# Swapping quarters of turned attention operands: GpSimd's copies in place of its transfers

## The chip, the cores and the metric

One core of one Trainium2 chip runs the kernel. The metric is device microseconds of one execution. The kernel before takes 556.05 us as the median of three runs (554.33 to 557.03).

## The reference

Sigmoid attention over 4 batches and 12 heads (448 positions, head size 64), then two gated MLPs with a spatial product, all in float32:

```python
scores = scale * np.matmul(q, k.transpose(0, 1, 3, 2)) - np.log(S)
attn = 1.0 / (1.0 + np.exp(-scores))
attn_out = np.matmul(attn, v)                    # then heads side by side: x is 4 x 448 x 768
h = np.maximum(x @ w_in, 0.0)                    # the first MLP; the second has gelu and g_ln
u, v = h[..., :512], h[..., 512:]
v_n = (v - mu) / np.sqrt(var + 1e-06)
v_s = np.einsum('ts,bsd->btd', w_spatial, v_n) + b_spatial[None, :, None]
x = (u * v_s) @ w_out                            # the second MLP returns x + (u * v_s) @ w_out
```

## The kernel before

The program runs in one order that is written out by hand: attention first (up to 137 us), then the first MLP, a merge of two weight matrices, and the second MLP. Only attention is touched.

Attention works on 12 groups of 4 heads. Each group has 7 units (chunks of 64 key positions), so there are 84 units, numbered s. Unit s does four score matmuls (`scores`, line 464) on four quarters of the systolic array, ScalarE takes the sigmoid (line 470), and three units later four matmuls apply the values (`values`, line 482).

The score matmuls need q and k with the head dimension on partitions. `turn(n)` (line 407) makes this for group n. VectorE transposes 32x32 blocks of the loaded tile `in` into two tiles `op0` and `op1` (line 398, four instructions). Block transposes leave quarters of 32 partitions in the wrong place, so both tiles are copied whole into two spare tiles `t0` and `t1` (line 416), and four quarters are then brought back to other partitions: `op0[32:64]` from `t1[0:32]`, `op1[0:32]` from `t0[32:64]`, and the same again 64 partitions on (`swaps`, line 400). For group 1 VectorE does these four copies (line 419). For groups 2 to 11 GpSimd's queue issues them as DMA transfers (line 421), forty in all. Group 0 has a path of its own, `turn_first`, which uses copies of VectorE, ScalarE and GpSimd (lines 434 to 441). Matmul `(x, o)` of a unit reads partitions 64o to 64o+63 of `op{x}`, in the order x0o0, x0o1, x1o0, x1o1.

`turn(1)` is issued at unit 0, `turn(n + 2)` at the third unit of group n. The `op` tiles have three buffers, the `t` tiles one: the whole copies of one turn (line 416) wait until the quarters of the turn before have been read out of `t`.

Between the turns VectorE works on a belt of 18 jobs (`convert_early`, line 162), which make float32 weights of MLP 1 out of float64 ones: load (line 168 or 170), five integer instructions (lines 175, 178, 181, 185, 190), then for 14 of them a rounded copy and a difference (lines 198, 199), and for the last four a store to `flat` in HBM (line 195). The order of VectorE's instructions is fixed, so a turn and the belt's jobs push each other. Tiles `we` and `fe` of the belt have three buffers each; SyncE issues the loads in order.

At the end of attention `operands_made` (line 850) closes the pool `apool`, which holds `in`, `op`, `t`, `we` and `fe`, and the MLP's pools take its space. The first instruction there (`split_x`, line 574, on ScalarE) makes the first operand of the MLP and waits for the last users of that space, the belt's last store among them. VectorE makes the lower halves (line 575).

Of the kernel before, what the change touches and what calls it, by code (L numbers as in the profile page):

```python
# [26 lines left out]
def tile_sigmoid_attention_two_gated_mlps(  # L27
# [32 lines left out]
    nc = tc.nc  # L60
# [292 lines left out]
    def attention(apool, epool, ps_att, ps_last, done):  # L353
# [27 lines left out]
        def operands(n):  # L381
            ops[n] = [
                apool.tile([P, 2, S], F32, tag=f"op{x}", name=f"op{x}", bufs=3) for x in range(2)
            ]
            return ops[n]

        def spares():
            return [apool.tile([P, 2, S], F32, tag=f"t{x}", name=f"t{x}", bufs=1) for x in range(2)]

        def transpose(t, w, src, j=0, chunks=slice(0, None)):  # L390
            src = src.rearrange("p (c j d) -> p j c d", c=TC, j=2)[:, j]
            dst = t[:, w]
            if w:
                src = src.rearrange("p (e c) d -> p c e d", c=KC)[:, chunks]
                dst = dst.rearrange("p (c t e) -> p c e t", c=KC, e=2)[:, chunks]
            else:
                dst = dst.rearrange("p (c t) -> p c t", c=TC)
            nc.vector.transpose(out=dst, in_=src)

        def swaps(ts, us):  # L400


            for at in (0, 64):
                yield ts[0][at + 32:at + 64], us[1][at:at + 32]
                yield ts[1][at:at + 32], us[0][at + 32:at + 64]

        def turn(n):


            ts = operands(n)  # L410
            for j, t in enumerate(ts):
                for w in range(2):
                    transpose(t, w, ins[n][:, w], j)
            us = spares()
            for t, u in zip(ts, us):
                nc.vector.tensor_copy(out=u, in_=t)
            for dst, src in swaps(ts, us):
                if n == 1:
                    nc.vector.tensor_copy(out=dst, in_=src)
                else:  # L420
                    nc.gpsimd.dma_start(out=dst, in_=src)  # L421

        def turn_first():

# [107 lines left out]
        for s in range(U + LAG):  # L532
            n, c = divmod(s, KC)
            if s < U:
                scores(n, c)
            elif s == U:
                done()
            if s in sums:
                values(*sums[s])
            if s == 0:  # L540
                turn(1)
            if c == 2 and n + 2 < NG:
                turn(n + 2)
            if c == 5 and n + 3 < NG:
                load(n + 3)
            if c == 0 and 0 < n < NG - 1:
                load_v(n + 1)
            if s % 2 == 0:
                belt.tick(rate(s // 14, s % 14 // 2))
            if s == U:  # L550
                load_vecs(l1)
            if s >= U and (s - U) % 2 == 0:
                spatial.tick(1)
# [504 lines left out]
```

## Time and profile before

| | us |
|---|---|
| median of three runs | 556.05 |
| lowest, highest | 554.33, 557.03 |
| the profiled execution | 553.84 |
| its span, first to last instruction | 552.1 |
| TensorE busy | 546.1 |
| VectorE busy | 343.8 |
| ScalarE busy | 220.4 |
| GpSimd busy | 55.4 |

The page of the profile gives busy time by engine and in 40 slices. The chain of work that ended last is followed back from the last instruction; the timeline gives the instructions of an engine in order of time, with the idle time before one and what ended it; the waits are summed by pairs of lines. The granted TensorE clock is 1.0 throughout.

### The profile page before, as it was taken

The page shows a single profiled execution, that of the slowest core. Times are in us where ns is not written, and L with a number is a line of the kernel's source. Part 1 is how long each engine was busy: PE and PEld are TensorE (multiplying, and loading weights), DVE is VectorE, ACT ScalarE, POOL GpSimd, SP SyncE. Part 2 cuts the span into 40 slices and gives each one's busy share as a digit, 9 for nine tenths or more (in the row PEclk, how much of TensorE's full clock was granted, in tenths as well). Part 3 has the DMA queues.
Part 4 walks back from the last instruction along what each step waited for, and adds up shares of the span by engine and source line. Part 5 has one row for each costly group of instructions (what it writes and reads, how often), then busy time and mean ns, then how long its engine had stood idle before and what let it go on. Part 6 is the DMA issues. An engine that isn't in the chain of part 4 may idle for free.

```text
span 552.1 us, 8964 instructions
## 1 busy us (share of the span) xinstructions
PE 546.1 (99%) x3398; PEld 448.5 (81%) x3398; DVE 343.8 (62%) x734; ACT 220.4 (40%) x371; POOL 55.4 (10%) x104
## 2 busy tenths in 40 slices
PE   8999999999999999999999999999999999999997
PEld 5356666666899898898998889998999899989886
DVE  6559788793588799999674877932541264225311
ACT  5767777878242352452533245311320142113001
POOL 1112121110210200201100021001000120010000
PEclk9999999999999999999999999999999999999999
DMA  8979989671422454452445534101410032014003
GB/s 281 276 192 243 257 248 263 185 197 52 65 76 96 101 157 116 137 146 88 136 138 117 138 119 132 55 2 20 64 17 1 16 53 33 1 20 67 1 0 115
DMA packets 89547, 61.02 MB, mean 111 GB/s; under 512 B 63776, under 2 KB 77088, under 8 KB 89504
## 3 DMA queue, kind: packets, MB, share of 16 engines
q1 hardware_dynamic: 88080, 55.60, 37.4%
q0 software_dynamic: 1280, 4.59, 3.6%
q8 instruction: 27, 0.44, 0.3%
q10 hardware_dynamic: 144, 0.26, 0.1%
q14 instruction: 16, 0.13, 0.1%
HBM read 44.83 MB, written 11.01 MB: 101 GB/s over the span
## 4 chain that ended last, share of the span: by engine, by line
PE 94%; DMA 3%; DVE 1%; SPq 0%; issue 0%; POOL 0%
PE t L587 17%; PE t L633 17%; PE sc L719 10%; PE av L482 10%; PE sc L464 10%; PE t L653 6%; PE av L719 5%; PE av L653 3%; PE sc L653 3%; PE sc L729 3%; PE t L815 3%; PE av L815 3%; PE av L729 2%; PE t L729 2%; DMA op<-t 1%; DMA in<-in_k_dram 1%
## 5 line engine op out<-in xcount | busy, mean ns | idle before, releaser
L464 PE MATMUL sc<-op 64*64 64x448 f32 x656 | 117.2, 536 | 0.9 <-DMA op<-t 0.9
L482 PE MATMUL av<-a,vt 64*64 64x448 f32 x672 | 118.0, 536 | 0.0
L470 ACT ACTIVATE a<-sc,small 128x896 f32<-128x896 f32 x84 | 84.8, 1013 | 33.9 <-PE sc L464 33.1
L464 PEld LDWEIGHTS sc<-op 64*64 64x64 f32 x656 | 53.2, 133 | 28.4 <-issue 7.1
L482 PEld LDWEIGHTS av<-a,vt 64*64 64x64 f32 x672 | 54.5, 133 | 25.8 <-issue 6.8
L596 DVE BATCH_NORM_STATS2 st<-vr 128x6 f32<-128x512 f32 x28 | 19.4, 694 | 65.2 <-ACT vr L593 65.2
L593 ACT ACTIVATE vr<-t 128x512 f32<-128x512 f32 x28 | 16.7, 598 | 92.6 <-PE t L587 92.5
L598 POOL TENSOR_SCALAR st<-st 128x1 f32<-128x1 f32 x28 | 10.8, 385 | 352.7 <-DVE st L597 322.6
L587 PE MATMUL t<-vh,xh 128*128 128x512 f32 x112 | 41.6, 392 | 0.0
L663 DVE SCALAR_TENSOR_TENSOR gt<-t,bb 128x448 f32<-128x448 f32 x16 | 10.9, 682 | 45.7 <-PE t L653 45.7
L587 PE MATMUL t<-vh,xl 128*128 128x512 f32 x98 | 38.2, 390 | 0.0
L671 ACT CAST gh<-u 128x448 fp32r<-128x448 f32 (+1 forms) x16 | 8.6, 540 | 71.8 <-DVE u L667 71.8
L633 PE MATMUL t<-xh,uh 128*128 128x448 f32 x96 | 34.8, 363 | 0.0
L633 PE MATMUL t<-xh,ul 128*128 128x448 f32 x96 | 34.8, 362 | 0.0
L633 PE MATMUL t<-xl,uh 128*128 128x448 f32 x96 | 34.6, 360 | 0.0
L653 PE MATMUL t<-sh,v 128*128 128x448 f32 x112 | 32.8, 362 | 0.0
L587 PE MATMUL t<-vl,xh 128*128 128x512 f32 x84 | 32.7, 389 | 0.0
L575 DVE TENSOR_TENSOR xl<-x,xh 128x512 fp32r<-128x512 f32 (+1 forms) x32 | 20.0, 654 | 17.1 <-ACT xh L574 16.9
L421 POOL DMA_DIRECT2D op<-t x40 | 21.7, 548 | 83.3 <-PE sc L464 55.0
L633 PE MATMUL t<-xh,vl 128*128 128x448 f32 x96 | 29.6, 362 | 0.0
L638 ACT ACTIVATE u<-t 128x448 f32<-128x448 f32 x32 | 17.4, 544 | 25.2 <-PE t L633 24.9
L615 ACT CAST v<-vr 128x512 fp32r<-128x512 f32 x24 | 14.9, 622 | 30.6 <-DVE vr L607 30.6
(200 smaller groups left out, 1246.4 us busy)
## 6 DMA issues: line engine op xcount, KB each, us to landing
w<-in_moe_w_in_dram SPq DMA_DIRECT2D x24, 256.0 KB, 3.0
in<-in_q_dram SPq DMA_DIRECT2D x12, 448.0 KB, 6.3
vt<-in_v_dram SPq DMA_DIRECT2D x12, 448.0 KB, 6.8
in<-in_k_dram SPq DMA_DIRECT2D x11, 448.0 KB, 7.1
w<-in_moe_w_out_dram SPq DMA_DIRECT2D x18, 256.0 KB, 3.1
op<-t POOLq DMA_DIRECT2D x40, 112.0 KB, 4.9
we<-in_moe_w_in_dram SPq DMA_DIRECT2D x12, 256.0 KB, 8.9
we<-in_moe_w_in_dram SPq DMA_DIRECT2D x16, 192.0 KB, 5.5
```

The lines of the kernel that those rows point to most:

```text
L421: nc.gpsimd.dma_start(out=dst, in_=src)
L464: nc.tensor.matmul(sc[64 * x:64 * x + 64, o, :S], op[x][ps, 1, 64 * c:64 * c + 64], op[x][ps, 0], start=(j == 0), stop=(j == js - 1), tile ...
L470: nc.scalar.activation(a, sc[..., :S], AF.Sigmoid, bias=bias_s, scale=scale)
L482: nc.tensor.matmul(av[o * D:(o + 1) * D, x, :S], vs[n][ps, o, D * c:D * (c + 1)], att[n, c][ps, o], start=(c == 0), stop=(c == KC - 1), ti ...
L575: nc.vector.tensor_tensor(out=pair[1][:, :n], in0=src, in1=raw(pair[0][:, :n]), op=ALU.subtract)
L587: nc.tensor.matmul(ps[:, :FF], a, w, start=(c == 0 and n == 0), stop=(c == self.kc - 1 and n == 2),)
L596: nc.vector.bn_stats(out=st, in_=vr)
L633: nc.tensor.matmul(ps[:, :S], w, a, start=(c == 0 and n == 0), stop=(c == self.kc - 1 and n == 2),)
L653: nc.tensor.matmul(ps[:, :S], a, w, start=(n == 0), stop=(n == len(todo) - 1))
L719: nc.tensor.matmul(self.o[m][:, :n_cols], w, a, start=(not second and i == 0 and n == 0), stop=(second and i == KF - 1 and n == 2),)
L729: nc.tensor.matmul(ps[:, :cols.stop - cols.start], a, w, start=(not second and i == 0 and n == 0), stop=(second and i == KF - 1 and n == 2),)
L815: nc.tensor.matmul(ps[:, :FF], x, w[:, c], start=(c == 0 and n == 0), stop=(c == KD - 1 and n == 2),)
```

## The change

For group 1, VectorE now copies the first and third quarter and GpSimd the second and fourth. For groups 2 to 11, GpSimd copies all four quarters with instructions of its own, and its forty transfers go. Everything else stays: the whole copies into `t`, the order, the buffers.

```diff
-            for dst, src in swaps(ts, us):
-                if n == 1:
-                    nc.vector.tensor_copy(out=dst, in_=src)
-                else:
-                    nc.gpsimd.dma_start(out=dst, in_=src)
+            for i, (dst, src) in enumerate(swaps(ts, us)):
+                engine = nc.vector if n == 1 and i % 2 == 0 else nc.gpsimd
+                engine.tensor_copy(out=dst, in_=src)
```

## Rows read from the trace of the kernel before

**Rows 1.** The page, busy us (share of the span) and instructions by engine.
```profile
PE 546.1 (99%) x3398; PEld 448.5 (81%) x3398; DVE 343.8 (62%) x734; ACT 220.4 (40%) x371; POOL 55.4 (10%) x104
```

**Rows 2.** Timeline of ScalarE: sigmoids of units 13, 14 and 83; start, us, idle before.
```profile
25.99 1.01 ACT L470 ACTIVATE a<-sc,small 128x896 f32<-128x896 f32 x1 [0.52 <-PE sc L464]
30.02 1.01 ACT L470 ACTIVATE a<-sc,small 128x896 f32<-128x896 f32 x1 [3.01 <-PE sc L464]
...
133.74 1.01 ACT L470 ACTIVATE a<-sc,small 128x896 f32<-128x896 f32 x1 [0.50 <-PE sc L464]
```

**Rows 3.** The chain that ended last: start, us, what.
```profile
20.39 7.76 DMA op<-t
```

**Rows 4.** Timeline, turns of groups 2 and 3 and TensorE's unit 14.
```profile
18.77 2.40 DVE L398 STREAM_TRANSPOSE op<-in 128x448 f32<-128x448 f32 x4
19.17 2.22 POOL L421 DMA_DIRECT2D op<-t  x4 [11.40 <-DVE t L416]
...
26.41 0.91 PE L464 MATMUL sc<-op 64*64 64x448 f32 x2
...
29.03 1.16 DVE L416 COPY t<-op 128x896 f32<-128x896 f32 x2 [7.85 <-DMA op<-t]
```

**Rows 5.** Waits, summed: total us, times, longest.
```profile
DVE t L416 <- DMA op<-t: 21.2, 5, 7.9
```

**Rows 6.** Timeline of VectorE: belt instructions behind a turn, and the last turn's copies.
```profile
61.14 0.69 DVE L190 SCALAR_TENSOR_TENSOR fe<-we,fe 128x512 int32<-128x512 int32 x1
61.86 0.43 DVE L198 CAST vh<-fe 128x512 fp32r<-128x512 f32 x1
...
62.93 0.42 DVE L175 TENSOR_SCALAR fe<-we 128x512 int32<-128x512 int32 x1
...
108.88 1.12 DVE L416 COPY t<-op 128x896 f32<-128x896 f32 x2
```

**Rows 7.** Timeline, the belt's end and the start of the MLP.
```profile
126.22 0.56 DVE L190 SCALAR_TENSOR_TENSOR fe<-we,fe 128x384 int32<-128x384 int32 x1
...
126.80 0.32 SPq L195 DMA_DIRECT2D flat<-fe  x1
...
134.65 2.16 ACT L574 CAST xh<-x 128x512 fp32r<-128x512 f32 x4
```

**Rows 8.** Waits of SyncE's queue up to 140 us, and line 195's landing time.
```profile
SPq L320 <- DMA flat<-fe: 1.4, 1, 1.4
...
DMA to landing us min/median/max: 1.8/2.2/3.4
```

**Rows 9.** Timeline in group 0, lines 398, 438 and 441, each copy by itself.
```profile
6.25 0.90 DVE L398 STREAM_TRANSPOSE t<-in 128x320 f32<-128x320 f32 x2
6.49 0.55 POOL L441 COPY op<-t 32x448 f32<-32x448 f32 x1 [5.19 <-DVE op L434]
7.07 0.28 DVE L438 COPY op<-t 128x320 f32<-128x320 f32 x1
7.09 0.68 POOL L441 COPY op<-t 32x448 f32<-32x448 f32 x1
```

**Rows 10.** Lines 438 and 598 by themselves: duration in ns, min/median/max.
```profile
L438 DVE COPY op<-t x2: 283/483/683, 7.1 to 7.3; 128x320 f32<-128x320 f32 x2
...
L598 POOL TENSOR_SCALAR st<-st x28: 221/422/582, 142.9 to 498.2; 128x1 f32<-128x1 f32 x28
```

**Rows 11.** Timeline of GpSimd and VectorE in MLP 1.
```profile
143.16 0.57 POOL L601 TENSOR_TENSOR st<-st,small 128x1 f32<-128x1 f32 x1
...
190.58 0.69 DVE L617 TENSOR_TENSOR v<-vr,v 128x512 fp32r<-128x512 f32 x1
...
190.83 0.87 POOL L601 TENSOR_TENSOR st<-st,small 128x1 f32<-128x1 f32 x1
```

**Rows 12.** Timeline, quarters of group 1 and TensorE's unit 7.
```profile
13.01 2.55 DVE L419 COPY op<-t 32x896 f32<-32x896 f32 x4
...
15.89 0.93 PE L464 MATMUL sc<-op 64*64 64x448 f32 x8
```

## The prediction

> **What bounds the kernel now.** The page first: TensorE is busy for 546.1 of 552.1 us [rows 1], so a change that touches only VectorE, GpSimd and transfers can win no more than TensorE's gaps, but it can open new ones. TensorE's ends are modelled; its gaps in attention are better read from ScalarE, whose sigmoids follow the score matmuls one by one. From unit 14 to unit 83 they start (133.74 - 30.02) / 69 = 1.503 us apart: no gap in 69 units. From unit 13 to unit 14 it is 4.03 us [rows 2]. So attention has one stall of 4.03 - 1.50 = 2.53 us. The chain names its cause: a transfer `op<-t` that ran from 20.39 to 28.15 [rows 3], the swap of group 2, while unit 14 had started its first two matmuls at 26.41 [rows 4].
>
> Then VectorE, which is off the chain. Its timeline is one queue of turns and belt jobs, and the only idle time it shows between 12 and 126 us is five waits of the whole copies (line 416) for the transfers, 21.2 us [rows 5], the longest 7.85 us [rows 4]. It ends its last belt instruction at 126.22 + 0.56 = 126.78; the store is issued at 126.80 [rows 7] and takes about 2.2 us to land [rows 8]: 129.0. The space of `apool` is handed on only then: SyncE's first load into it stood 1.4 us for that store [rows 8]. The first MLP operand starts at 134.65 [rows 7], behind the last sigmoid. VectorE's lateness is thus free up to 134.65 - 129.0 = 5.6 us, and after that it moves the end of attention one for one.
>
> **The change, part by part. Prices.** GpSimd copied 32x448 in 0.55 us beside transposes, and in 0.68 us when a VectorE copy had started just before it. Two VectorE copies of 128x320 lay there: the first took 283 ns, the second, issued while GpSimd copied, 683 ns, so it stood 0.40 us [rows 9, 10]. A GpSimd copy and such a VectorE copy go one after the other here; the transposes (0.90 us for two, beside the first GpSimd copy) did not slow it. The new copies are 32x896, twice as long: 2 x 0.55 = 1.10 us if all of it is per element; if a fixed part as long as GpSimd's shortest one-column instruction, 0.22 us [rows 10], is in it, 0.22 + 2 x 0.33 = 0.88 us. I take 1.0 us.
>
> **The stall of group 2 goes.** The whole copies of group 2 ended about 18.9; four GpSimd copies of 1.0 us end near 22.9, beside transposes only [rows 4]. Unit 14 asks at 26.41, so even (26.41 - 18.9) / 4 = 1.9 us each would do. All later turns start earlier than before, as VectorE's waits shrink too (below). Worth 2.53 us.
>
> **Group 1 loses a little.** VectorE's four copies run from 13.01 to 15.56 and unit 7 starts at 15.89 [rows 12]. Now VectorE and GpSimd take turns: VectorE 13.01, GpSimd from about 13.5, VectorE from 14.4, GpSimd from about 14.9 to 15.9. The fourth quarter then comes 0 us (no turns taken: 13.05 + 2 x 1.0 = 15.05) to 0.6 us late (1.1 us each and turns taken); I take 0.25. TensorE's side of the sum is -2.53 + 0.25 = -2.3 us: the MLP could start at 132.35.
>
> **VectorE's side.** Gone: 21.2 us of waits, and 0.5 us in group 1 (two copies fewer, one wait more). New: the whole copies of group 3 wait for group 2's quarters to be read from `t`, until 22.5, where the transposes are done near 20.7: 1.8 us. Behind them on VectorE stand the belt and all later turns. Without collisions the belt would end at 126.78 - 21.2 - 0.5 + 1.8 = 106.9 at the earliest.
>
> Collisions: behind the copies of each later turn stand belt instructions [rows 6], in part copies and one-input integer instructions (0.43 us for 512 columns, at the copies' speed), in part two-input ones (0.69 us). Does a two-input instruction exclude GpSimd too? A GpSimd instruction of one column takes 0.57 us beside a transpose and 0.87 us where a two-input VectorE instruction of 0.69 us had begun 0.25 us before it [rows 11]; so GpSimd stands behind them. That VectorE's two-input instructions stand behind GpSimd's in turn, no row shows; I take it as symmetric. The Trainium skill (SBUF — State Buffer, "Who interferes with whom") says so: a VectorE instruction with two SBUF inputs contends with a GpSimd instruction that reads SBUF, and the later one blocks fully. By that rule the sum is the one made here; if it did not hold, the first rival below would be.
>
> So VectorE and GpSimd alternate until the four copies are through. Each copy costs VectorE 2 x 0.40 = 0.80 us (0.40 + 0.33 = 0.73 with the fixed part; 0.93, twice the 0.46 us for which the second GpSimd copy kept VectorE out, as the upper end). Group 2's copies lie beside transposes, at nothing; group 3's are followed by four belt instructions and meet three; groups 4 to 11 meet four each: 3 + 32 = 35 collisions, 28.0 us (25.5 to 32.5). The belt ends at 106.9 + 28.0 = 134.9, its store lands at 137.1, and the MLP's first operand starts there and not at 132.35: 137.1 - 134.65 = +2.5 us (0 to +7.0).
>
> On the way the last turn is just in time: its whole copies, before until 110.0 [rows 6], end at 110.0 - 21.2 - 0.5 + 1.8 + 31 x 0.80 = 114.9, its quarters some 5.4 us later at 120.3, and unit 77 asks at 30.02 + 63 x 1.503 - 1.1 - 2.3 = 121.3. The belt's end, not a turn, is what comes last.
>
> The forty transfers leave the DMA engines; TensorE waits for no other load in attention, so this is worth nothing.
>
> **Sum.** 553.84 + 2.5 = 556.3 on the profiled execution (553.8 to 560.8). That execution is 2.2 us under the median. What makes the others longer is not in the trace; if it were later landings of the swaps, it would go, and if not, it stays. I add 0.7: **557.0 us**.
>
> **The rivals.** (1) Two-input instructions don't stand behind GpSimd. Then only lines 198, 175, 178 and 181 collide, with about half of each copy hidden under the others: some 2.1 us a turn, 18 us in all. The belt ends near 125, its store lands by 127.3, under 132.35, and the whole gain stays: 553.84 - 2.3 = 551.5, up to 553.7 with the median's 2.2. For it: VectorE has 26.8 us of room (21.2 + 5.6) ahead of any loss. Against it: the 0.87 us. Chance 0.28. (2) GpSimd's next copy takes the turn as soon as the last ends, and VectorE stands through all four, 4.2 us a turn, 38 us over nine turns: the belt ends near 145, and the MLP starts 12 us late, 566. For it: GpSimd's copies are queued ready; against it: at 7.09 GpSimd got in between two VectorE copies that were equally ready [rows 9]. It decides from 0.85 us a collision on, where the sum passes 558.8. Chance 0.10. (3) The swap is no earlier than by transfer, and the stall of group 2 stays; it needs copies of 1.9 us, nearly twice any row. Then 558.8 or more. Chance 0.02.
>
> **How the numbers follow.** My own case has 0.60. About 0.5% (2.8 us) is what a measurement of this kernel can tell from no change: faster is under 553.3, slower over 558.8. My case gives 0.38 to no change, 0.19 to slower (its upper bounds, and the 2.2 us if common), 0.03 to faster; rival 1 gives 0.19 to faster, 0.09 to no change; rivals 2 and 3 give 0.12 to slower; together, rounded, 0.22, 0.47 and 0.31. The range runs from rival 1 at its best, 551.5, to my upper end with half of the median's surplus, 562; what is left out is rival 2 and the outer ends.
>
> **What would show it.** Right: GpSimd copies of 0.9 to 1.1 us alone and longer beside belt work; belt instructions of 0.43 and 0.69 us stretched to 1.2 to 1.5 us behind each turn; sigmoids 13 and 14 1.5 us apart; the last store after 132 us and the first `xh` waiting for it. Wrong: lines 185, 190 and 199 keep their durations beside GpSimd copies (rival 1), VectorE stands for 3 us at a stretch (rival 2), or TensorE waits inside attention at a later group.

## The result and the profile after

| | before | after |
|---|---|---|
| median, us | 555.54 (6 executions, 554.14 to 558.12) | 551.28 (6 executions, 550.64 to 551.56) |
| the profiled execution, us | 553.84 | 551.56 |
| its span, us | 552.1 | 549.8 |
| TensorE busy, us | 546.1 | 545.0 |
| VectorE busy, us | 343.8 | 364.8 |
| GpSimd busy, us | 55.4 | 79.2 |

The ratio of after to before is 0.9917, 95% interval 0.9891 to 0.9944: faster by 0.8%. The forecast was 557.0, no change or slower. The time came out 0.2 us below the range. (In after.py the lines behind 419 stand 2 lower: sigmoid L468, score matmul L462, first MLP operand L572. The quarters are L419. In e2 and e3 below, the lines from the quarters on stand 2 higher than in before; in e6 most stand 1 lower.)

The page of after, busy time by engine:

```profile
PE 545.0 (99%) x3398; PEld 439.8 (80%) x3398; DVE 364.8 (66%) x732; ACT 220.3 (40%) x371; POOL 79.2 (14%) x106
```

VectorE became 21.0 us busier [rows 1] and the kernel faster. TensorE's busy time fell by 1.1 us of the 2.3 us by which the span fell; its ends are modelled, so the gaps are read from ScalarE.

**Where it went: the gap between units 13 and 14.** Timeline of ScalarE in after, units 13 and 14 (start, duration):

```profile
26.48 1.01 ACT L468 ACTIVATE a<-sc,small 128x896 f32<-128x896 f32 x1 [0.50 <-PE sc L462]
27.99 1.01 ACT L468 ACTIVATE a<-sc,small 128x896 f32<-128x896 f32 x1 [0.50 <-PE sc L462]
```

1.51 us apart where it was 4.03 [rows 2]. The quarters of group 2 now lie on GpSimd, beside transposes. Timelines of GpSimd and VectorE there:

```profile
18.92 3.87 POOL L419 COPY op<-t 32x896 f32<-32x896 f32 x4 [2.57 <-DVE t L416]
...
18.77 2.27 DVE L398 STREAM_TRANSPOSE op<-in 128x448 f32<-128x448 f32 x4
22.82 1.16 DVE L416 COPY t<-op 128x896 f32<-128x896 f32 x2 [1.78 <-POOL op L419]
```

The four copies end at 22.79, 5.4 us before the transfer did [rows 3], and the score matmuls of unit 14 start at 27.14. VectorE's wait of 7.85 us at the next whole copies [rows 4] became 1.78 us. It is the only wait of that kind that is left, in place of 21.2 us [rows 5].

**What it costs on VectorE.** Timeline of VectorE in after, belt instructions behind a turn in the middle of attention, to be held against [rows 6]:

```profile
53.93 0.69 DVE L190 SCALAR_TENSOR_TENSOR fe<-we,fe 128x512 int32<-128x512 int32 x1
54.65 1.04 DVE L198 CAST vh<-fe 128x512 fp32r<-128x512 f32 x1
55.72 1.29 DVE L199 TENSOR_TENSOR vl<-fe,vh 128x512 fp32r<-128x512 f32 x1
56.94 1.15 DVE L175 TENSOR_SCALAR fe<-we 128x512 int32<-128x512 int32 x1
58.12 1.04 DVE L178 TENSOR_SCALAR fe<-fe 128x512 f32<-128x512 f32 x1
59.20 0.43 DVE L181 TENSOR_SCALAR fe<-fe 128x512 int32<-128x512 int32 x1
```

Four instructions in a row are stretched, one for each GpSimd copy, and the fifth is not: the two engines take turns. The stretch is read against the lone durations (0.43, 0.69, 0.42, 0.43): 0.61 + 0.60 + 0.73 + 0.61 = 2.55 us a turn. The forecast had 4 x 0.80 = 3.2. Counted over the whole timeline, 35 belt instructions are stretched, three behind group 3's copies and four behind those of each later group, by 22.4 us together.

**Where it ends.** VectorE's last belt instruction, and the MLP's first operand on ScalarE behind the last sigmoid (timelines of after); then, from its chain, TensorE's last value matmuls and first MLP matmuls:

```profile
128.40 0.56 DVE L190 SCALAR_TENSOR_TENSOR fe<-we,fe 128x384 int32<-128x384 int32 x1
...
131.72 1.01 ACT L468 ACTIVATE a<-sc,small 128x896 f32<-128x896 f32 x1 [0.50 <-PE sc L462]
132.62 2.17 ACT L572 CAST xh<-x 128x512 fp32r<-128x512 f32 x4
...
131.62 3.01 PE av L480 x32
134.63 5.44 PE t L585 x23
```

The belt ends at 128.96. Its store takes 2.1 us to land (1.8 to 2.3 for the four of them): 131.1. That is 1.5 us before the last sigmoid makes room for the first `xh`, so nothing waits for the belt, and the MLP's first operand starts 134.65 - 132.62 = 2.03 us earlier than before [rows 7]. TensorE is busy with the values of the last units until 134.63, 2.0 us behind the first `xh`; only then do its MLP matmuls begin, without a gap.

### The profile page after: what moved, and what is told of

It reads as the page before. It is cut to its first block, busy times and chain, and to the rows that moved or that the text cites. A ratio compares the mean times of both kernels' runs of the same rounds, so it can differ in the third digit from the quotient of the medians.

```text
span 549.8 us, 8932 instructions
## 1 busy us (share of the span) xinstructions
PE 545.0 (99%) x3398; PEld 439.8 (80%) x3398; DVE 364.8 (66%) x732; ACT 220.3 (40%) x371; POOL 79.2 (14%) x106
## 4 chain that ended last, share of the span: by engine, by line
PE 99%; POOL 0%; DVE 0%; issue 0%; POOLq 0%
PE t L585 18%; PE t L631 17%; PE sc L462 12%; PE av L480 12%; PE sc L717 10%; PE t L651 6%; PE av L717 5%; PE av L651 3%; PE sc L651 3%; PE sc L727 3%; PE t L813 3%; PE av L813 3%; PE av L727 2%; PE t L727 2%; PE av L529 1%; DVE x L779 0%
## 5 line engine op out<-in xcount | busy, mean ns | idle before, releaser
L480 PE MATMUL av<-a,vt 64*64 64x448 f32 x672 | 101.3, 536 | 0.0
L462 PE MATMUL sc<-op 64*64 64x448 f32 x656 | 99.6, 536 | 0.0
L468 ACT ACTIVATE a<-sc,small 128x896 f32<-128x896 f32 x84 | 84.8, 1013 | 31.9 <-PE sc L462 31.1
L480 PEld LDWEIGHTS av<-a,vt 64*64 64x64 f32 x672 | 38.9, 133 | 30.8 <-issue 30.1
L462 PEld LDWEIGHTS sc<-op 64*64 64x64 f32 x656 | 38.2, 133 | 30.1 <-issue 29.1
L596 POOL TENSOR_SCALAR st<-st 128x1 f32<-128x1 f32 x28 | 10.8, 385 | 349.2 <-DVE st L595 322.5
L419 POOL COPY op<-t 32x896 f32<-32x896 f32 x42 | 45.5, 1083 | 61.0 <-DVE t L416 59.3
```

Of the source, the lines that this page charges most:

```text
L419: engine.tensor_copy(out=dst, in_=src)
L462: nc.tensor.matmul(sc[64 * x:64 * x + 64, o, :S], op[x][ps, 1, 64 * c:64 * c + 64], op[x][ps, 0], start=(j == 0), stop=(j == js - 1), tile ...
L468: nc.scalar.activation(a, sc[..., :S], AF.Sigmoid, bias=bias_s, scale=scale)
L480: nc.tensor.matmul(av[o * D:(o + 1) * D, x, :S], vs[n][ps, o, D * c:D * (c + 1)], att[n, c][ps, o], start=(c == 0), stop=(c == KC - 1), ti ...
```

## The experiments

The theory after the result: the gain is the late swap of group 2 alone, and whatever in the longer executions of before comes from late swaps; the price is one stretched VectorE instruction for each GpSimd copy, and it is paid in room that VectorE has, so it shows only once the belt's store is late. Its rivals: the gain comes from all groups; the two other microseconds of the median have another cause; a collision costs 0.80 us after all and something else made up for it.

### What made the other executions of before longer

Two more profiles of the kernel before, unchanged (e1 and e8).

> The kernel before, unchanged, profiled once more. Its first profiled execution took 553.84 us and had one stall in attention, 2.53 us ahead of the sigmoid of unit 14; its timed executions went up to 558. Theory A, the surplus is late landing of the quarters' transfers: this execution's time above 551.3 is the sum of the gaps between sigmoids over 1.50 us, within 0.5 us, and they lie at the first unit of a group (14, 21 or 35), behind a transfer. Rival B, the surplus lies elsewhere: the stall is again near 2.5 us whatever the time, and the rest of the time is found in the start or in the MLPs.

> The kernel before, unchanged, profiled a third time. As for the second profile: if late transfers make the surplus, the time above 551.3 us is the sum of the gaps between sigmoids over 1.50 us; if not, the gap at unit 14 stays near 2.5 us and the rest is elsewhere.

The first took 555.55 us. Timeline of ScalarE, units 34 and 35 (group 5), and VectorE's wait at that place:

```profile
60.67 1.01 ACT L470 ACTIVATE a<-sc,small 128x896 f32<-128x896 f32 x1 [0.50 <-PE sc L464]
63.30 1.01 ACT L470 ACTIVATE a<-sc,small 128x896 f32<-128x896 f32 x1 [1.62 <-PE sc L464]
...
62.32 1.16 DVE L416 COPY t<-op 128x896 f32<-128x896 f32 x2 [4.32 <-DMA op<-t]
```

and the two transfers in its chain:

```profile
32.60 7.29 DMA op<-t
53.70 7.71 DMA op<-t
```

The gaps beyond 1.50 us, at units 14, 21, 28 and 35, are 2.44 + 0.38 + 0.13 + 1.13 = 4.08 us, and 555.55 - 4.08 = 551.47. The second took 554.67 us with gaps of 3.56 us at units 7, 14, 21, 28 and 35 (the 0.36 of unit 7 is a late load of `in`): 551.11. The first profile had 2.53: 553.84 - 2.53 = 551.31. Three executions of different length stand on one floor of 551.1 to 551.5, which is the time of after. So in these two the surplus over the first profile is gaps at later groups, nearly all of them late swaps. That is not shown for the longer executions: the medians beside these two profiles were 557.07 and 555.17 us, and none above 555.6 was traced. In 15 of the 58 executions of before that were timed with the experiments the mean granted clock is 0.994 to 0.997, in all of after 0.999 or 1.0; what that costs no trace of before shows (e3 shows one such case). That the surplus goes as a whole when the swap of group 2 is on time is shown by e2.

### Group 2 alone, and all groups but group 2

Group 2 alone (e2):

```diff
                     nc.vector.tensor_copy(out=dst, in_=src)
+                elif n == 2:
+                    nc.gpsimd.tensor_copy(out=dst, in_=src)
                 else:
```

> Only group 2's quarters are copied by GpSimd; groups 3 to 11 keep the transfers, group 1 stays on VectorE. If the stall of group 2 is all that the change removes: 551.0 to 551.6 us, as the change or 0.25 us better (group 1 is not split), with a spread as narrow as the change's. If part of the 4 us of the medians comes from later groups whose transfers land late in some executions: a median of 552 to 554 and a spread of 2 us or more.

551.67 us median of 5 (550.96 to 552.01); ratio to before 0.9906, interval 0.9885 to 0.9926. The whole gain, with 36 of the 40 transfers still there. VectorE waits on for them (waits of this kernel, summed):

```profile
DVE t L416 <- DMA op<-t: 18.7, 5, 7.4
```

18.7 us of waiting off TensorE's path cost nothing: the sigmoids of the profiled execution show no gap, and its belt ends at 125.84. The later groups' swaps are as slow as before, but with group 2 on time none of them came late in the profiled execution, and the five lie within 1.05 us of each other.

The counterpart (e3) changes `n == 2` to `n > 2`:

> Groups 3 to 11 are copied by GpSimd, group 2 keeps its transfers, group 1 stays on VectorE. If only group 2's stall counts: as the kernel before, 553.8 to 556, with a stall of some 2.5 us at unit 14 in the profile. VectorE then starts late, behind the wait for group 2's transfers (7.85 us), and still loses some 22 us in collisions: its belt ends near 134 and the MLP's first operand starts at 136 or later, 1 to 2 us later than before, so up to 557. If later groups' transfers make the spread, it goes: 553.5 to 554.5.

556.47 us median of 12 (554.17 to 558.94); ratio 0.9996, interval 0.9977 to 1.0016. Nothing gained. Its profiled execution, of 558.04 us, shows both ends of the theory. The swap of group 2 in the chain and the sigmoid of unit 14; the last belt instruction, the first `xh` and the first MLP matmul; and the view of the stretch from 140 to 141 us, in which the third number from the end is the granted TensorE clock:

```profile
21.32 8.26 DMA op<-t
...
30.69 1.01 ACT L472 ACTIVATE a<-sc,small 128x896 f32<-128x896 f32 x1 [3.56 <-PE sc L466]
...
135.36 0.56 DVE L190 SCALAR_TENSOR_TENSOR fe<-we,fe 128x384 int32<-128x384 int32 x1
138.23 2.18 ACT L576 CAST xh<-x 128x512 fp32r<-128x512 f32 x4 [2.80 <-DMA flat<-fe]
138.90 0.50 PE L589 MATMUL t<-vh,xh 128*128 128x512 f32 x1 [1.57 <-ACT xh L576]
...
140.00:141.00 1.00, 1.00 (x3) 0.79 (x3) 1.00 (x3) 1.00 (x3) 0.00 (x0) 0.50 0.48 118
```

Here VectorE pays both, a wait of 8.3 us for group 2's transfer and the collisions of groups 3 to 11. The belt ends at 135.92, and ScalarE's first `xh` stands 2.80 us for its store. TensorE stands only 1.57 us, as it still has values to work on and its first MLP matmul follows the first `xh` by 0.67 us. But behind this idle stretch the granted clock is 0.50, the lower of its two levels (1.2 of 2.4 GHz), and its first 72 MLP matmuls take longer than before's. From the chains of e3 and of before:

```profile
138.90 18.47 PE t L589 x72
```

```profile
136.65 16.54 PE t L587 x72
```

That is 1.93 us more. The gap before unit 14 is 3.56 - 0.50 = 3.06 us, 0.53 more than in before; no later unit has one. With 0.11 us of a later start this makes 0.11 + 0.53 + 1.57 + 1.93 = 4.14 of the 4.20 us by which this execution is longer than before's first profile. That is the loss that the prediction feared, in a kernel that does not have the gain. So e3 does not show that the later groups are worth nothing: their gaps are gone, and the late belt takes that back.

### Where the room on VectorE ends

A fifth copy in groups 3 to 11, of a quarter already copied (e5):

```diff
                 engine.tensor_copy(out=dst, in_=src)
+            if n > 2:
+                nc.gpsimd.tensor_copy(out=dst, in_=src)
```

> The change with a fifth GpSimd copy in groups 3 to 11 (the last quarter is copied twice). Theory: VectorE's collisions cost nothing only as long as the belt's last store lands before the last sigmoid ends; in the change the belt ends at 128.96 and the first MLP operand starts at 132.6. One collision more for each of groups 4 to 11, at 0.62 us, is 5.0 us: the belt ends near 134.0, its store lands near 136.1, and the MLP starts 3.5 us later: 554.8 us. Rival, VectorE's lateness doesn't reach the path (another wait holds the first operand, or VectorE finds slack elsewhere): 551.3, no change.

554.94 us median of 10 (552.90 to 555.78), ratio to before 0.998, interval 0.9961 to 0.9999, near the 554.8 expected, though the profiled execution took 1.9 us less than that. A fifth instruction in a row is stretched now, and the MLP waits. Timelines of VectorE, ScalarE and TensorE in this kernel:

```profile
59.52 1.03 DVE L181 TENSOR_SCALAR fe<-fe 128x512 int32<-128x512 int32 x1
...
132.35 0.56 DVE L190 SCALAR_TENSOR_TENSOR fe<-we,fe 128x384 int32<-128x384 int32 x1
...
134.92 2.18 ACT L574 CAST xh<-x 128x512 fp32r<-128x512 f32 x4 [2.38 <-DMA flat<-fe]
135.59 0.50 PE L587 MATMUL t<-vh,xh 128*128 128x512 f32 x1 [1.18 <-ACT xh L574]
```

The belt ends at 132.91 and `xh` starts 2.01 us later. In e3 it is 2.31 us. So for ScalarE the limit is the one that the prediction named, the belt's end and a store of about 2.2 us; the change stays 1.5 us short of it. For TensorE, which sets the time, it lies some 2.0 - 0.67 = 1.3 us further. ScalarE stands 2.38 us here and TensorE 1.18, and the first MLP matmul comes 0.96 us later than in after, where the expectation had 3.5. So it is luck that the median agrees with 554.8. The profiled execution was the shortest of the ten. In five of the others the mean granted clock is 0.997, as in e3's profiled execution, and their spans are 553.1 to 554.0 us; the five at 0.999 or 1.0 have 551.1 to 552.1. A fall of the clock behind the wait, worth 1.9 us in e3, would fit; none of the five was traced, so this is not shown.

### Group 1 on VectorE

The change without the split of group 1 (e4):

```diff
-                engine = nc.vector if n == 1 and i % 2 == 0 else nc.gpsimd
+                engine = nc.vector if n == 1 else nc.gpsimd
```

> The change, but with group 1's four quarters on VectorE as before. The sigmoid of unit 7 came 0.25 us later (counted from unit 0) with the split than without. If that is what the split costs: 0.25 us faster than the change, 551.0, and units 6 to 7 as in the kernel before. If the split saves VectorE's time where it matters: equal or slower than the change.

551.21 us median of 4 (550.60 to 551.69), not told apart from the change by its median. Timeline of ScalarE, units 5, 6 and 7 (a row with x2 is units 5 and 6), first after, then this kernel:

```profile
14.87 1.91 ACT L468 ACTIVATE a<-sc,small 128x896 f32<-128x896 f32 x2 [0.49 <-PE sc L462]
17.46 1.01 ACT L468 ACTIVATE a<-sc,small 128x896 f32<-128x896 f32 x1 [0.68 <-PE sc L462]
```

```profile
14.59 1.90 ACT L468 ACTIVATE a<-sc,small 128x896 f32<-128x896 f32 x2 [0.50 <-PE sc L462]
16.93 1.01 ACT L468 ACTIVATE a<-sc,small 128x896 f32<-128x896 f32 x1 [0.44 <-PE sc L462]
```

2.59 us against 2.34: unit 7 came 0.25 us later in after, the value that the prediction took. But this is not the price of the split. VectorE's transposes of group 1 had stood for loads of `in` in after, which they did not in e4; and e10 is after once more, without such a wait. Timeline of VectorE in after, then of ScalarE in e10, units 5, 6 and 7:

```profile
9.79 0.65 DVE L398 STREAM_TRANSPOSE op<-in 128x448 f32<-128x448 f32 x1 [0.48 <-DMA in<-in_q_dram]
10.89 1.71 DVE L398 STREAM_TRANSPOSE op<-in 128x448 f32<-128x448 f32 x3 [0.46 <-DMA in<-in_k_dram]
```

```profile
14.21 1.91 ACT L468 ACTIVATE a<-sc,small 128x896 f32<-128x896 f32 x2 [0.50 <-PE sc L462]
16.60 1.01 ACT L468 ACTIVATE a<-sc,small 128x896 f32<-128x896 f32 x1 [0.49 <-PE sc L462]
```

2.39 us in e10: the split costs 0.05 us, and the rest of the 0.25 was a late load.

### What one collision costs

Each quarter as two copies of 448 columns, on the engine that does it in after (e6):

```diff
-                engine.tensor_copy(out=dst, in_=src)
+                for w in range(2):
+                    engine.tensor_copy(out=dst[:, w], in_=src[:, w])
```

> The change with each quarter copied as two halves of 448 columns, eight GpSimd copies a turn. This prices one collision with the size that stood in the trace of before, where VectorE stood 0.40 us. Theory 1, GpSimd keeps VectorE out for 0.46 us with 448 columns and 0.80 us with 896, and 0.19 us of that lies under the tail of the belt instruction in front: belt instructions are stretched by 0.27 us each, 2.2 us a turn, the belt ends some 3 us earlier, 551.3 us. Theory 2, each stretch is 0.40 us as in the trace of before: 3.2 us a turn, the belt ends 5 us later, the MLP starts some 3.5 us later, 554.8 us.

550.96 us median of 6 (550.73 to 552.97), ratio 0.9926, interval 0.9901 to 0.9951. Timeline of VectorE behind the same turn:

```profile
53.42 0.67 DVE L198 CAST vh<-fe 128x512 fp32r<-128x512 f32 x1
54.12 0.92 DVE L199 TENSOR_TENSOR vl<-fe,vh 128x512 fp32r<-128x512 f32 x1
54.96 0.78 DVE L175 TENSOR_SCALAR fe<-we 128x512 int32<-128x512 int32 x1
...
58.12 0.93 DVE L190 SCALAR_TENSOR_TENSOR fe<-we,fe 128x512 int32<-128x512 int32 x1
59.08 0.67 DVE L198 CAST vh<-fe 128x512 fp32r<-128x512 f32 x1
```

Eight instructions in a row are stretched, one for each copy, seven of them by 0.23 to 0.24 us and L175 by 0.36, not by the 0.40 us that a 448-column copy had cost in group 0 [rows 10]. The lone durations of the two copies, by the shortest of line 419 in after and of the same copies in this kernel (min, median, max in ns):

```profile
L419 POOL COPY op<-t x42: 926/1032/1378, 13.7 to 113.2; 32x896 f32<-32x896 f32 x42
```

```profile
L420 POOL COPY op<-t x84: 550/726/1015, 12.7 to 109.8; 32x448 f32<-32x448 f32 x84
```

0.926 - 0.61 = 0.31 and 0.550 - 0.24 = 0.31: here a collision costs VectorE the lone duration of the GpSimd copy less 0.31 us, at both lengths. So halving the columns cuts the price from 0.61 to 0.24, and the eight half copies of this turn cost VectorE 2.0 us where four whole ones cost 2.55. Over all of attention it is 15.4 us in 61 stretches, where after has 22.4 in 35. The belt ends at 123.96, 5.0 us earlier than after. It brings no time, as the belt is not what comes last; it is room.

### The quarters on VectorE

No copies on GpSimd (e7):

```diff
-                engine = nc.vector if n == 1 and i % 2 == 0 else nc.gpsimd
+                engine = nc.vector
```

> All quarters of groups 1 to 11 on VectorE, GpSimd does none. VectorE's four quarters took 2.55 us for group 1; the collisions with GpSimd's copies cost it 2.57 us a turn in the change. If the only price of GpSimd's copies is what they take from VectorE: the belt ends 2.55 x 10 - 22.4 - 1.8 = 1.3 us later than in the change, at 130.3, its store lands at 132.5, just in time: 551.0 to 551.5 us, no slower than the change. Rival, GpSimd's copies are done beside VectorE at a gain: the belt ends past 134 and the time is 554 or more.

552.14 us median of 11 (551.65 to 553.63), ratio 0.9946, interval 0.9926 to 0.9965: a miss, some 0.6 to 1.1 us over what was expected. Timelines of VectorE (a turn's four quarters, the belt behind them, the last belt instruction) and of ScalarE:

```profile
57.05 2.55 DVE L419 COPY op<-t 32x896 f32<-32x896 f32 x4
59.63 0.69 DVE L190 SCALAR_TENSOR_TENSOR fe<-we,fe 128x512 int32<-128x512 int32 x1
...
132.26 0.56 DVE L190 SCALAR_TENSOR_TENSOR fe<-we,fe 128x384 int32<-128x384 int32 x1
...
134.85 2.18 ACT L572 CAST xh<-x 128x512 fp32r<-128x512 f32 x4 [1.79 <-DMA flat<-fe]
```

Four copies cost VectorE 2.58 us a turn when it makes them and 2.55 when GpSimd does. GpSimd saves VectorE nothing in a turn that is followed by belt work; it saves the whole of group 2, where its copies lie beside transposes. The expectation had put the belt's end at 130.3, not 132.82, and so did not see the store come late; it had left out group 1, where VectorE's copies take 2.55 us instead of 1.89. In the profiled execution ScalarE stands 1.79 us for the store, and TensorE 0.56.

### More room for the transfers

The spare tiles twice, the transfers kept (e9):

```diff
-            return [apool.tile([P, 2, S], F32, tag=f"t{x}", name=f"t{x}", bufs=1) for x in range(2)]
+            return [apool.tile([P, 2, S], F32, tag=f"t{x}", name=f"t{x}", bufs=2) for x in range(2)]
```

> The kernel before, with two buffers of the spare tiles t instead of one; all quarters of groups 2 to 11 still by transfer. VectorE's whole copies of a turn then wait for the quarters of the turn before last. Theory: the late swap of group 2 costs twice, directly (2.2 to 2.5 us at unit 14) and through VectorE, which stands 7.4 to 7.9 us for it and is late with the turns of groups 3, 4 and 5 (0.1 to 1.1 us each at units 21, 28 and 35 in the second and third profiles). With two buffers the second part goes: gaps at units 21 to 35 under 0.1 us each, the gap at unit 14 still 3.7 to 4.1 us, time 553.3 to 554, spread under 1.5 us. Rival, the later gaps come from transfers that are late by themselves: the median stays at 555 to 557 and the gaps remain.

555.17 us median of 12 (553.39 to 558.44), ratio 0.9978, interval 0.9954 to 1.0002: a miss, by the median and by the spread. VectorE's waits for transfers did go. Its waits, summed; the time from issue to landing of the quarters' transfers; and the late transfer of the chain with the sigmoid of unit 63:

```profile
DVE fe L175 <- DMA we<-in_moe_w_in_dram: 10.8, 7, 3.1
DVE op L398 <- DMA in<-in_k_dram: 8.5, 7, 1.6
DVE t L416 <- DMA op<-t: 0.5, 1, 0.5
...
DMA to landing us min/median/max: 4.9/8.7/11.6
...
93.29 10.11 DMA op<-t
...
105.00 1.01 ACT L470 ACTIVATE a<-sc,small 128x896 f32<-128x896 f32 x1 [1.80 <-PE sc L464]
```

From 21.2 us to 0.5, with no gap at units 21, 28 and 35. But VectorE now stands 10.8 and 8.5 us for its loads instead, group 2's gap stays (2.12 us), and the transfers land later: 8.7 us behind their issue in the median, where before's three profiles have 4.9, 5.7 and 5.6. One of group 9 took 10.11 us and cost 1.31 us at unit 63; it also belonged to a turn whose transfers were issued from 92.28 on, 1.8 us later than in before (90.46), as VectorE had stood 1.3 us for a load of `in`. So later gaps have two causes, turns that start late and transfers that land late. The second was not expected. Why the landing times rose was not tested; from 20 to 60 us the DMA share is 1.04 here and 0.91 in before.

### The change again, and both refinements together

The first (e10) is the change, unedited. The second (e11) has group 1 on VectorE, as in e4, and half copies on GpSimd, as in e6:

```diff
-            for i, (dst, src) in enumerate(swaps(ts, us)):
-                engine = nc.vector if n == 1 and i % 2 == 0 else nc.gpsimd
-                engine.tensor_copy(out=dst, in_=src)
+            for dst, src in swaps(ts, us):
+                if n == 1:
+                    nc.vector.tensor_copy(out=dst, in_=src)
+                    continue
+                for w in range(2):
+                    nc.gpsimd.tensor_copy(out=dst[:, w], in_=src[:, w])
```

> The change, unchanged, as the measure for the variants on the same chip: 551.0 to 551.6 us, no stall but 0.25 us at unit 7.

> Group 1 on VectorE as before, groups 2 to 11 by GpSimd in halves of 448 columns. The split of group 1 cost 0.25 us at unit 7; the halves gave VectorE back 5 us ahead of the last store, which are room and no time. So 0.25 us faster than the change on the same chip, 550.8 to 551.3, and the belt ends near 124.

551.48 us median of 6 (550.59 to 552.04), ratio 0.9906 (0.9882 to 0.9930), and 551.14 median of 6 (550.64 to 551.82), ratio 0.9903 (0.9876 to 0.9929). The gain repeats. The 0.25 us that both expectations took for group 1 are 0.05 in e10, as shown at e4, and the second is not shown to be faster than the change.

## Why the prediction was wrong

**Right: what bounds the kernel, and TensorE's side.** One gap of 2.53 us before unit 14 goes: e2 and e3 show that group 2 carries the gain. That the sum of -2.3 us meets the 551.56 - 553.84 = -2.28 us between the two profiled executions is in part luck: the 0.25 us taken for group 1 came from a late load, where the split costs 0.05, and after's first sigmoid also came 0.24 us later, which the rest of the program made up.

**Right: the shape of VectorE's side.** Group 2 at nothing beside transposes, three collisions in group 3, four in each of the eight later groups, a wait of 1.8 us and engines that take turns: each is in the trace of after. (The two times behind the wait, 20.7 and 22.5, were both some 0.4 us early; their difference held.) That the belt's store can come last is shown by e3, e5 and e7, where the first `xh` waits for it and the belt ends after 132 us.

**Right: two-input instructions stand behind GpSimd's copies.** Line 199, with two inputs, went from 0.69 to 1.29 us behind a turn, like its one-input neighbours. That kills rival 1 as a mechanism, though the time came out near its number. By the rule that the Trainium skill gives (SBUF — State Buffer, "Who interferes with whom"), a VectorE instruction with two SBUF inputs contends with a GpSimd instruction that reads SBUF; the trace of after agrees, 0.60 us for line 199 behind a copy of 896 columns.

**Wrong: the price of one collision.** This is the step that failed: "Each copy costs VectorE 2 x 0.40 = 0.80 us". It measured 0.60 to 0.73 in the turn shown, mostly 0.61. The three of group 3 cost 1.82 us (1.04, 1.03 and 1.30 us for lines 178, 181 and 185) and a later turn 2.55 to 2.58: 1.82 + 8 x 2.57 = 22.4 us where the sum had 28.0. With it the forecast's own working gives 106.9 + 22.4 = 129.3 for the belt's end, against 128.96 measured. The row was the wrong neighbour: 0.40 us is what a GpSimd copy of 448 columns cost a VectorE copy in group 0, and behind belt instructions the same size costs 0.24 (e6). Doubling it for twice the columns does not hold either, as part of the price does not grow with them: 0.24 went to 0.61, not to 0.48. The two errors pulled opposite ways. Why the copies of group 0 paid 0.16 more is open.

What made a misjudged 0.16 us decide the case is a margin that the text did not work out. By its own numbers the MLP can start on time up to (132.35 - 2.2 - 106.9) / 35 = 0.66 us a collision. The forecast lay at 0.80 and its lower bound at 0.73; the truth lay at 22.4 / 35 = 0.64. The lower bound was itself wrong: the price was doubled out of one row, and no row bounded it from below. With 22.4 us in place of 28.0 its sum is 553.84 - 2.3 + 0.7 = 552.2 us: of the 5.7 us by which the forecast missed, 4.8 are this term.

**Wrong, without being decisive: a late store moves the end of attention "one for one".** It does so for ScalarE's first operand. TensorE has some 1.3 us more, as its last values run on (e3, e5, e7), so its limit is 0.70 us a collision, and the forecast's own loss of 2.5 us would have been about 1.2. In the other direction, the prediction put nothing for the clock, which in e3 fell behind such a wait and cost 1.93 us.

**Wrong: the median's surplus.** Of the 2.2 us a guess of 0.7 was added to the sum, as a loss that stays. None of it stayed: the median fell by 4.3 us where the profiled execution fell by 2.3, and in e2, with group 2 alone, by 5.4 (557.07 to 551.67). e1 and e8 show late swaps as its cause in two executions; for the longest it is not shown. The prediction had named this possibility and had no row for it, as one profile shows one execution.

## What to carry to other kernels

Before a sum of many equal small costs decides between two signs, work out at what unit price it turns, and see whether the row behind the price is known that well; here it turned at 0.66, and the price was known to no better than 0.2. When the executions of a kernel spread more than its gaps explain, ask which of its waits is for something whose latency varies, and credit its removal with the spread. A late operand at one place can carry the whole of a change made at eleven. Price a wait at the engine that sets the time: the same late store held ScalarE for 2.38 us and TensorE for 1.18. And work put on an idle engine is not free if it makes the busy one wait: try it where the neighbours do not collide.

## What the hardware showed

A GpSimd copy of 32x896 float32 (0.93 us alone) makes a waiting VectorE instruction 0.61 us longer, one of 32x448 (0.55 us alone) 0.24 us, so shorter copies cost less in all (15.4 against 22.4 us). Transposes beside GpSimd's copies were not slowed: four took 2.27 us beside group 2's copies, and 2.40 beside its transfers [rows 4].

The same kind of transfer within a core, one quarter, took 7.2 to 8.3 us where it stood on the chain of before's three profiles and of e3, and 10.11 us in e9. Group 2's was late in each profile where it was a transfer; the later groups 3 to 5 came late in e1 and e8 and not in before's first profile.
